# A two-layer decode kernel: second-layer P.V with V moving, another order in the last round, and another closing MLP

## The chip, the cores and the metric

The kernel runs on one core of a Trainium2 chip. The metric is the device time of one execution in microseconds (us), lower is better. The core has five engines with queues of their own: PE (TensorE; its weight loads are shown apart as PEld), DVE (VectorE), ACT (ScalarE), POOL (GpSimd) and SP (SyncE), which here only issues DMAs. They wait for each other by semaphores.

## What is computed

Two identical decoder layers in sequence, for 8 sequences of one new token each, both layers over the same K and V cache and with the same weights:

```python
def _A_ref(x, k_cache, v_cache, wq, wo):          # x: 8 x 1 x 512
    q = (x @ wq).reshape(B, 1, 32, 128).transpose(0, 2, 1, 3)
    k = jnp.repeat(k_cache, 4, axis=1)            # cache: 8 x 8 heads x 8192 x 128
    v = jnp.repeat(v_cache, 4, axis=1)
    p = _softmax(jnp.einsum("bhqd,bhkd->bhqk", q, k) * 128 ** -0.5)
    o = jnp.einsum("bhqk,bhkd->bhqd", p, v)
    return o.transpose(0, 2, 1, 3).reshape(B, 1, 4096) @ wo

def _B_ref(x, w1, w2):                            # 512 -> 1792 -> 512
    return _silu(x @ w1) @ w2

x = x + _A_ref(_layernorm(x), k_cache, v_cache, wq, wo)
x = x + _B_ref(_layernorm(x), w1, w2)
x = x + _A_ref(_layernorm(x), k_cache, v_cache, wq, wo)
x = x + _B_ref(_layernorm(x), w1, w2)
```

All inputs are bf16. K and V of one sequence and one KV head are 2 MB each; the 64 of them make 134 MB of K and 134 MB of V, and both layers need all of it.

## The kernel before

**Tasks.** A task is (layer, batch b, KV head g): 128 in all. Its 8192 keys are cut into 4 granules of 512 KB (k = 0 to 3) of two halves each, so a task has 8 half-granules; the main loop counts them with `p`, 8 positions a task. A half-granule is 8 chunks of 128 keys.

**The arena.** `ARENA` holds 28 slots of one granule (512 KB). For heads 3 to 7 (`first` = 3) the K granules of the batch in turn stay in 20 home slots from the first-layer task to the second-layer task, transposed: such a *kept* second-layer task loads only V and transposes no K. Everything else streams through the slots that are free.

**The order.** `make_tasks` writes it: per batch b the five kept first-layer tasks, then `HIDE` = 4 other tasks (first-layer tasks of later batches, second-layer tasks of heads 0 to 2 of earlier ones), in whose shadow the chain of batch b runs (wo, layer norm, w1, silu, w2, layer norm, wq: `chain_of`), then the five kept second-layer tasks `c[b]`, then what is left of that round. In the last round (b = 7) all of the other tasks stand ahead of `c[7]`, and the three second-layer tasks of heads 0 to 2 of batch 7 close the kernel. `plan_loads` then makes a list of loads, of 1, 2 or 4 granules by the table `WIDTHS` and by how tight the slots are, each with a slot and the position after which it may be issued; SP issues them in that order, each waiting for its slot.

**One position** (loop at the end of `_build`), in the order of emission: `emit_q` at the end of the task before; `emit_t` for position p + 1 (K not kept: 8 transposes on PE into a PSUM bank, and one copy of 128x1024 back into the arena, on ACT for the half-granules in `ACT_EVAC` and on DVE for the others); at odd p `emit_s`, the scores of a granule: four products of 512 columns, each with 32 output rows, into the four quarters of one PSUM bank; at even p `emit_pv` for two half-granules 12 positions back. The softmax of a task runs in the first positions of the next one: position 0 the maximum (DVE, POOL), 1 the shift and the exponential (DVE, ACT, into `P`), 3 the sum and `emit_pt` (four transposes of P on PE, one DVE copy into `PT`), 7 the reciprocal. P.V begins at position 4. `emit_norm` multiplies the result by the reciprocal, 18 positions after the task's first.

**P.V before** (`emit_pv`): V is the stationary operand. Each chunk of 128 keys is loaded as weights (128x128) and a few columns of `PT` move through it, repeated to 64 (heads 3 to 7) or 48 columns; 64 such products a task accumulate in a PSUM bank `OTp`, whose columns are then the wanted 128 (features) x 4 (query heads).

**The closing.** When the last task is done, `closing` does batch-wide wo residual, layer norm, MLP and the output: means by PE (`means`), x minus mean into `xbB` (DVE), w1 on that (`project`), squares and their sum over partitions (ACT, DVE, POOL), the inverse root by Ln and Exp on ACT, a table load (`load_table(SILU)`), the scaling (DVE), silu (ACT), w2 on PE into the bank that already holds x, a copy to `P`, and four output DMAs. `keep_busy` issues products whose result nobody reads.

Of the kernel before, what the change touches and what calls it, by code (L numbers as in the profile page):

```python
# [13 lines left out]
GRP = 8  # L14
GPT = 8
# [10 lines left out]
HIDE = 4  # L26
WIDTHS = {
# [35 lines left out]
SILU = 18  # L63
ACT_EVAC = (1, 4, 6)

# [105 lines left out]
def make_tasks(nb, nkv, keep_from):  # L171
# [11 lines left out]
    for b in range(nb):  # L183
        if b:
            tasks += kept[b]
        size = -(-(2 * first * (nb - 1)) // nb) if b in (0, nb - 1) else 2 * first * (nb - 1) // nb
        must = max(0, first * min(b + 1, nb - 1) - na)
        nd = size if b == nb - 1 else min(len(behind), first, size - must)
        more = behind[:nd] + ahead[na:na + size - nd]
        del behind[:nd]  # L190
        na += size - nd
        if b + 1 == nb:
            more += behind
        hide = len(more) if b + 1 == nb else HIDE
        tasks += more[:hide] + c[b] + more[hide:]
        behind += d[b]
# [14 lines left out]
def plan_loads(tasks, kept, nslot, ngran):  # L211
# [29 lines left out]
    def phase(i):  # L241
        if i >= len(tasks) - ENDING:
            return None
# [4 lines left out]
        if j < 0:  # L248
            return None
# [78 lines left out]
def _build(ctx, nc, A_x, A_k_cache, A_v_cache, A_wq, A_wo, B_w1, B_w2, out):  # L328
# [29 lines left out]
    def sb(shape, dt, name):  # L358
        _cnt[0] += 1
        return ctx.enter_context(nc.sbuf_tensor(f"{name}_{_cnt[0]}", shape, dt))  # L360
# [38 lines left out]
    PT = PTb[:, :].rearrange("p (x q) -> p x q", q=NQ * USED)  # L399
# [3 lines left out]
    small = sb([128, 4 * B + 4 * REP * NST + USED + 2 * FT + 2 * HQ + NST + 1 + halves], FP32, "small")  # L403
    taken = [0]
# [91 lines left out]
    with nc.Block() as block:  # L496

        @block.sync
        def _(sync_eng):
# [29 lines left out]

            queue = list(loads)  # L530
# [23 lines left out]

            evacs = [0]
# [11 lines left out]
            def emit_t(i):  # L567
# [11 lines left out]
                if i % GPT in ACT_EVAC:  # L579
# [69 lines left out]
            def emit_pt(ti):  # L649
# [9 lines left out]
                    PT.rearrange("p x (c q) -> p x c q", q=USED),  # L659
                    tpv.rearrange("p x (c q) -> p x c q", q=QUAD)[:, :, :, 0:USED]),  # L660
# [6 lines left out]
            def emit_pv(i):  # L667
# [4 lines left out]
                pv = PT.rearrange("p x (c r k) -> p x c k r", c=NQ, k=NGRAN)  # L672
# [12 lines left out]

            def width_of(ti):
                return PVN[(tasks[ti][2], NGRAN - 1) in kept]

            def emit_norm(ti):
# [4 lines left out]
                else:  # L694
                    dst, rd = QA[:, b * HQ + g * REP:b * HQ + (g + 1) * REP], f"QA{b}"
                op(dve, lambda: dve.tensor_tensor(dst, OTp[ob][:, 0:REP * width_of(ti):width_of(ti)], rcp[st], ALU.mult),
                   reads=[f"OT{ob}", f"rcp{st}"], writes=[rd])
# [119 lines left out]
            def closing(x0, x1, r0, r1):  # L817
# [3 lines left out]
                def quads(lhs_of, rhs_of, parts, first, last):  # L821
# [5 lines left out]
                        for k in range(parts) for c in range(KT)  # L827
# [6 lines left out]
                mm_group(quads(lambda k, c: x1[:, c, :], lambda k, c: ident[:, :], 1, True, False),  # L834
                         reads=[r1, "ident"], writes=["SC0"])
# [4 lines left out]
                   reads=["s1"], writes=["s1a"])  # L840
                op(dve, lambda: dve.scalar_tensor_tensor(
                    xbB, means[:, 0:B].unsqueeze(1).to_broadcast([128, KT, B]), -1.0 / D, x1, op0=ALU.mult, op1=ALU.add),
                   reads=["SC1", r1], writes=["PT", "xb"])
                project(w1_sb, "w1", range(FT), KT, lambda k: xbB[:, k, :], "xb", B, again=AGAIN)[0]()
                keep_busy(AFTER)
# [7 lines left out]
                load_table(SILU)  # L853
                scaled(hB.rearrange("p (f b) -> p f b", b=B), ["P"], FT, AGAIN)
                op(act, lambda: act.activation(hsB, hB, ACT.Silu), reads=["P"], writes=["hsB"])
# [106 lines left out]
            LQ = 1  # L962
            soft = {0: [softmax_max], 1: [softmax_shift, softmax_exp], 3: [softmax_sum, emit_pt], 7: [softmax_rcp]}
# [12 lines left out]
            ntask = len(tasks)  # L976

            for p in range(NG + LP + GPT + 1):
# [36 lines left out]
                if done >= 0 and done % GPT == 0 and done // GPT < ntask:  # L1015
                    tj = done // GPT
                    emit_norm(tj)
# [52 lines left out]
```

## Time and profile before

| what | value |
|---|---|
| time, median of 3 runs | 1159.66 us (1158.61 to 1160.57) |
| the profiled execution: its time | 1162.76 us |
| the profiled execution: its span (first to last instruction) | 1161.0 us |
| busy: PE / PEld / DVE / ACT / POOL | 83% / 66% / 51% / 33% / 10% of the span |
| moved by DMA | 467.96 MB, 403 GB/s on the mean |
| chain that ended last, by engine | DMA 55%, PE 33%, DVE 4%, ACT 3% |
| mean granted PE clock | 0.956 |

Groups that the change touches, as the page lists them (line, engine, operation, shapes and count; busy us, mean ns of one; idle time before, with what ended it): the products of `emit_pv` (L679), 8192 in all, are busy 321.1 us with 191 ns on the mean; those of `emit_s` (L613), 2048, 213.1 us and 404 ns; the copy into `PT` (L658), 128, 37.3 us and 291 ns; the copies of K on ACT (L580), 264, 267.1 us and 1012 ns; `emit_norm` (L696), 128 of about 152 ns.

How to read it: a busy time is the time in which at least one instruction of the group was running; products on PE overlap, so 191 ns is the length of one from start to end and not the spacing. "Idle before" of an engine that has nothing to do costs nothing. In a timeline line the first number is the start in us from the first instruction, the second the length, and what stands in brackets is how long the engine sat idle before and who released it. Chains name the last thing waited for.

### The profile page before, as it was taken

The numbers are of one execution on the slowest core, as the hardware profiler recorded it, in microseconds if no ns is written. First come the engines' busy times: TensorE is split into PE (matmuls) and PEld (weight loads), VectorE is DVE, ScalarE is ACT, GpSimd is POOL, SyncE is SP. The second block draws the span as 40 slices with busy tenths as digits, with TensorE's granted clock in tenths as the row PEclk, the third lists the DMA queues.
The fourth block names the chain that finished last, engine by engine and source line by source line (L and its number), as shares of the span: only waits on it lengthen the run. The fifth ranks groups of instructions, "written<-read, shape, count | busy, mean of one in ns | idle before, by whom it ended". The sixth has DMA issues, their size and how long they took to land.

```text
span 1161.0 us, 44754 instructions
## 1 busy us (share of the span) xinstructions
PE 969.4 (83%) x19900; PEld 762.2 (66%) x19904; DVE 595.4 (51%) x1936; ACT 387.9 (33%) x663; POOL 117.3 (10%) x299
## 2 busy tenths in 40 slices
PE   4688888898879887889789888898789887898787
PEld 3476766677657765677567766676567666677566
DVE  3345654556445554556445654556355554556434
ACT  1233322343134332443134422343144322343223
POOL 0000010001101011001100110001100011011010
PEclk8789998999989999999989998899999989999999
DMA  9999999999999999999999999999999999999996
GB/s 365 387 422 409 397 414 423 420 395 399 416 423 416 354 409 426 421 402 403 422 422 409 392 412 426 410 399 407 423 417 414 368 390 425 422 391 408 410 414 239
DMA packets 87137, 467.96 MB, mean 403 GB/s; under 512 B 9112, under 2 KB 13216, under 8 KB 63776
## 3 DMA queue, kind: packets, MB, share of 16 engines
q1 hardware_dynamic: 86896, 465.08, 99.0%
q8 instruction: 157, 2.57, 0.9%
q14 instruction: 36, 0.29, 0.1%
q10 hardware_dynamic: 48, 0.01, 0.0%
HBM read 465.05 MB, written 0.01 MB: 401 GB/s over the span
## 4 chain that ended last, share of the span: by engine, by line
DMA 55%; PE 33%; DVE 4%; ACT 3%; issue 3%; SPq 2%; POOL 1%; POOLq 0%; ACTq 0%
DMA arena<-in_A_k_cache_dram 40%; DMA arena<-in_A_v_cache_dram 14%; PE TPp L574 13%; PE OTp L679 9%; PE SCp L613 6%; PE MISC L780 3%; SPq L468 2%; PE TPp L654 2%; ACT arena L580 1%; ACT P L638 1%; PE MISC L799 1%; DVE small L624 1%; DVE PT L658 1%; POOL small L628 1%; DVE arena L582 1%
## 5 line engine op out<-in xcount | busy, mean ns | idle before, releaser
L574 PE MATMUL TPp<-ident,arena 128*128 128x128 bf16 x5632 | 453.3, 226 | 91.2 <-DMA arena<-in_A_k_cache_dram 87.1
L582 DVE COPY arena<-TPp 128x1024 bf16<-128x1024 bf16 x440 | 304.1, 691 | 310.3 <-PE TPp L574 309.2
L574 PEld LDWEIGHTS TPp<-ident,arena 128*128 128x128 bf16 x5632 | 338.7, 101 | 153.7 <-DMA arena<-in_A_k_cache_dram 99.0
L580 ACT COPY arena<-TPp 128x1024 bf16<-128x1024 bf16 x264 | 267.1, 1012 | 441.7 <-PE TPp L574 441.1
L679 PE MATMUL OTp<-PT,arena 128*128 128x64 bf16 (+1 forms) x8192 | 321.1, 191 | 37.9 <-DMA arena<-in_A_v_cache_dram 17.1
L679 PEld LDWEIGHTS OTp<-PT,arena 128*128 128x128 bf16 x8192 | 278.7, 99 | 73.8 <-issue 46.5
L613 PE MATMUL SCp<-arena,QB 128*32 128x512 bf16 x2048 | 213.1, 404 | 17.6 <-ACT arena L580 11.1
L638 ACT ACTIVATE P<-SCp,small 128x512 bf16<-128x512 f32 x128 | 87.9, 687 | 222.1 <-DVE small L634 155.5
L628 POOL PARTITION_ALL_REDUCE small<-small x128 | 47.5, 371 | 691.6 <-DVE small L626 658.4
L613 PEld LDWEIGHTS SCp<-arena,QB 128*32 128x32 bf16 x2048 | 55.9, 94 | 67.5 <-DVE small L626 14.9
L624 DVE TENSOR_REDUCE small<-SCp 128x1 f32<-128x512 f32 x128 | 85.7, 670 | 22.6 <-PE SCp L613 21.9
L658 DVE COPY PT<-TPp 128x256 bf16<-128x256 bf16 x128 | 37.3, 291 | 88.8 <-PE TPp L654 88.7
L646 POOL PARTITION_ALL_REDUCE small<-small x128 | 55.9, 436 | 265.5 <-DVE small L644 265.5
L654 PE MATMUL TPp<-ident,P 128*128 128x128 bf16 x512 | 51.3, 223 | 22.1 <-ACT P L638 21.9
L654 PEld LDWEIGHTS TPp<-ident,P 128*128 128x128 bf16 x512 | 29.1, 98 | 54.6 <-ACT P L638 36.0
L780 PE MATMUL MISC<-XT,wq 128*128 128x32 bf16 x1024 | 41.2, 178 | 0.8 <-issue 0.8
L605 ACT COPY QB<-QT 128x4 bf16<-128x4 bf16 x64 | 12.9, 201 | 85.7 <-DVE QT L915 85.7
L780 PEld LDWEIGHTS MISC<-XT,wq 128*128 128x128 bf16 x1024 | 32.9, 96 | 10.6 <-issue 10.6
L644 DVE TENSOR_SCALAR small<-small 128x4 f32<-128x4 f32 x128 | 28.7, 224 | 19.8 <-ACT P L638 19.5
L894 DVE SCALAR_TENSOR_TENSOR small<-small,MISC 128x4 f32<-128x4 f32 (+1 forms) x64 | 13.9, 218 | 45.6 <-PE MISC L780 45.2
L799 PE MATMUL MISC<-at,wo 128*128 128x32 bf16 x1024 | 34.6, 176 | 0.5 <-issue 0.5
L799 PEld LDWEIGHTS MISC<-at,wo 128*128 128x128 bf16 x1024 | 31.0, 96 | 4.4 <-issue 3.1
(79 smaller groups left out, 342.4 us busy)
## 6 DMA issues: line engine op xcount, KB each, us to landing
arena<-in_A_v_cache_dram SPq DMA_DIRECT2D x240, 512.0 KB, 8.1
arena<-in_A_v_cache_dram SPq DMA_DIRECT2D x90, 1024.0 KB, 12.4
arena<-in_A_k_cache_dram SPq DMA_DIRECT2D x40, 2048.0 KB, 16.4
arena<-in_A_k_cache_dram SPq DMA_DIRECT2D x144, 512.0 KB, 8.1
arena<-in_A_v_cache_dram SPq DMA_DIRECT2D x23, 2048.0 KB, 14.2
arena<-in_A_k_cache_dram SPq DMA_DIRECT2D x24, 1024.0 KB, 10.6
wq<-in_A_wq_dram SPq DMA_DIRECT2D x1, 4096.0 KB, 16.8
wo<-in_A_wo_dram SPq DMA_DIRECT2D x1, 4096.0 KB, 27.9
```

Source lines behind the costliest of these rows:

```text
L574: lambda c=c: pe.transpose(tpv[:, c, :], chunk(slot, h * GRP + c), ident[:, :])
L580: op(act, lambda: act.copy(dst, TPp[tb][:, :]), reads=[f"TP{tb}"], writes=[r_half(slot, h)])
L582: op(dve, lambda: dve.tensor_copy(dst, TPp[tb][:, :]), reads=[f"TP{tb}"], writes=[r_half(slot, h)])
L613: lambda c=c: pe.matmul(SCp[bank][c * QUAD:(c + 1) * QUAD, :], QB[qn][:, NGRAN - 1 - k:NGRAN - 1 - k + QUAD], ARENA[:, slot * SLOT + c * K ...
L624: op(dve, lambda: dve.tensor_reduce(rowmax, SCp[bank][:, :], AX.X, ALU.max), reads=[f"SC{bank}"], writes=["rowmax"])
L628: op(pool, lambda: pool.partition_all_reduce(tops, top, 128, bass.bass_isa.ReduceOp.max), reads=["top"], writes=["tops"])
L638: op(act, lambda: act.activation(P[:, :], SCp[bank][:, :], ACT.Exp, bias=shift, scale=SM_SCALE, accum_out=rs[st]), reads=[f"SC{bank}", "sh ...
L646: op(pool, lambda: pool.partition_all_reduce(ssa[st], ssm[st], 128, bass.bass_isa.ReduceOp.add), reads=[f"ssm{st}"], writes=[f"ssa{st}"])
L654: lambda c=c: pe.transpose(tpv[:, c, :], P[:, c * 128:(c + 1) * 128], ident[:, :])
L679: lambda c=c, cc=cc: pe.matmul(otp, chunk(slot, h * GRP + c), pv[:, cc % CPB, cc // CPB % NQ, k, :].unsqueeze(2).to_broadcast([128, REP, w ...
L780: lambda i=i, o=o, k=k: pe.matmul(MISC[:, i * n:i * n + w] if again == 1 else MISC[:, i * w:(i + 1) * w].rearrange("p (r b) -> p r b", b=n ...
L799: lambda o=o, h=h: pe.matmul(MISC[:, o * w:(o + 1) * w], wo_sb[:, h, o * 128:(o + 1) * 128], rhs_of(h).to_broadcast([128, w]) if n == 1 el ...
```

## The change

Four things, in one diff.

1. **P.V of the kept second-layer tasks** (`tiled`): now PT is the stationary operand (16 columns: 4 chunks x 4 query heads) and V moves, 512 columns (4 chunks x 128 features) a product. There are two products a half-granule, each with its own quarter of the output rows; over the four granules they accumulate. Of each 16 x 512 block only the four 4 x 128 blocks on the diagonal are wanted. `gather` copies half of the bank (256 float32 columns) to SBUF with ACT, twice; `turned` multiplies each 128-column piece, in float32, with a matrix of zeros and ones (`pick`), which picks the rows, sums the four quarters and turns the result to features x query heads, in a score bank that is free at that time. `emit_norm` reads it there, at position 7 of the task instead of position 2 (`SPLIT` = 3: copy, product, copy, product at positions 3, 4, 5, 6). `PT` gets another layout, for all tasks. The K copies on ACT of the two tasks after a tiled one are those of half-granules 1, 4, 7 instead of 1, 4, 6.
2. **The last round**: only four tasks stand ahead of `c[7]`, as in the other rounds; the other two, (1, 6, 1) and (1, 6, 2), come after it. With that the planner's list changes from its 512th entry on: 553 loads instead of 564 (512 KB: 368 instead of 384; 1 MB: 116 instead of 114; 2 MB: 66 instead of 63).
3. **The closing**: w1 runs on x itself, and the mean is taken off afterwards with the column sums of w1 (`col1`, which the kernel has already); silu is h / (1 + exp(-h)), with Exp on ACT and the sum, the reciprocal and the product on DVE; the table load is gone.
4. `phase` gives names (`last1`, `start1`, ...) where it gave None; `WIDTHS` has no entry under these names, so no load changes by that.

```diff
+LASTHIDE = 4
...
-SILU = 18
 ACT_EVAC = (1, 4, 6)
+XW = 4
+SPLIT = 3
+TILED_EVAC = (1, 4, 7)
...
-        hide = len(more) if b + 1 == nb else HIDE
+        hide = LASTHIDE if b + 1 == nb else HIDE
...
+    pick = sb([128, XW * REP], FP32, "pick")
...
+            op(dve, lambda: dve.tensor_reduce(
+                    pick[:, :], ident[:, :].rearrange("p (c q) -> p q c", q=QUAD)[:, 0:XW * REP, :], AX.X, ALU.add), ...)
+            for n in range(2):
+                op(dve, lambda n=n: dve.memset(OTp[n][:, :], 0.0), writes=[f"OT{n}"])
...
-                if i % GPT in ACT_EVAC:
+                if i % GPT in (TILED_EVAC if i // GPT >= 2 and tiled(i // GPT - 2) else ACT_EVAC):
...
-                    PT.rearrange("p x (c q) -> p x c q", q=USED),
-                    tpv.rearrange("p x (c q) -> p x c q", q=QUAD)[:, :, :, 0:USED]),
+                    PT.rearrange("p (c k x r) -> p x c r k", c=NQ, k=NGRAN, r=REP),
+                    tpv.rearrange("p x (c q) -> p x c q", q=QUAD)[:, :, :, 0:USED].rearrange("p x c (r k) -> p x c r k", k=NGRAN)),
...
+                if tiled(ti):
+                    steps = []
+                    for n in range(GRP // XW):
+                        cc = h * GRP + n * XW
+                        at = (cc // CPB * (NGRAN - 1) + k) * CPB * REP
+                        tile = h * (GRP // XW) + n
+                        steps.append(
+                            lambda cc=cc, at=at, tile=tile: pe.matmul(
+                                OTp[ob][tile * QUAD:tile * QUAD + XW * REP, 0:XW * 128],
+                                PT[:, at + cc * REP:at + (cc + XW) * REP],
+                                ARENA[:, slot * SLOT + cc * 128:slot * SLOT + (cc + XW) * 128],
+                                start=(k == 0), stop=(k == NGRAN - 1),
+                            )
+                        )
+                    mm_group(steps, reads=[r_half(slot, h), "PT"], writes=[f"OT{ob}"])
+                    return
...
+            def tiled(ti):
+                return tasks[ti][0] == 1 and tasks[ti][2] >= first
+
+            def gather(ti, n, _bank):
+                ob = ti % 2
+                op(act, lambda: act.copy(Pf[:, :], OTp[ob][:, n * 256:(n + 1) * 256]), reads=[f"OT{ob}"], writes=["P"])
+
+            def turned(ti, n, bank):
+                mm_group(
+                    [lambda x=x: pe.matmul(SCp[bank][:, 0:REP], Pf[:, (x % 2) * 128:(x % 2 + 1) * 128],
+                                           pick[:, x * REP:(x + 1) * REP], start=(x == 0), stop=(x == XW - 1))
+                     for x in (2 * n, 2 * n + 1)], reads=["P", "pick"], writes=[f"SC{bank}"])
...
 # closing
+                project(w1_sb, "w1", range(FT), KT, lambda k: x1[:, k, :], r1, B, again=AGAIN)[0]()
+                mm_group(quads(lambda k, c: x1[:, c, :], lambda k, c: ident[:, :], 1, True, False), ...)
+                keep_busy(AFTER)
                 op(dve, lambda: dve.scalar_tensor_tensor(
-                    xbB, means[:, 0:B].unsqueeze(1).to_broadcast([128, KT, B]), -1.0 / D, x1, op0=ALU.mult, op1=ALU.add), ...)
-                project(w1_sb, "w1", range(FT), KT, lambda k: xbB[:, k, :], "xb", B, again=AGAIN)[0]()
-                keep_busy(AFTER)
+                    ev, means[:, 0:B].unsqueeze(1).to_broadcast([128, FT, B]), -1.0 / D,
+                    col1.unsqueeze(2).to_broadcast([128, FT, B]), op0=ALU.mult, op1=ALU.mult), ...)
...
-                load_table(SILU)
-                scaled(hB.rearrange("p (f b) -> p f b", b=B), ["P"], FT, AGAIN)
-                op(act, lambda: act.activation(hsB, hB, ACT.Silu), reads=["P"], writes=["hsB"])
+                op(dve, lambda: dve.tensor_tensor(hv, MISC[...], ev, ALU.add), ...)
+                op(dve, lambda: dve.tensor_tensor(hv, hv, yr[...], ALU.mult), ...)
+                op(act, lambda: act.activation(ehB, hB, ACT.Exp, scale=-1.0), reads=["P"], writes=["eh"])
+                op(dve, lambda: dve.tensor_scalar(ehB, ehB, 1.0, None, op0=ALU.add), ...)
+                op(dve, lambda: dve.reciprocal(ehB, ehB), reads=["eh"], writes=["eh"])
+                op(dve, lambda: dve.tensor_tensor(hsB, hB, ehB, ALU.mult), ...)
...
 # main loop
+            parts = XW // 2
+            rows_at = {SPLIT + 2 * n + m: (f, n) for n in range(parts) for m, f in enumerate((gather, turned))}
+            finish = SPLIT + 2 * parts
...
-                if done >= 0 and done % GPT == 0 and done // GPT < ntask:
-                    tj = done // GPT
-                    emit_norm(tj)
+                tj, d = done // GPT, done % GPT
+                split = 0 <= tj < ntask and tiled(tj)
+                bank = (tj + 1) % NSCP if split else None
+                if split and d + GPG in rows_at:
+                    f, n = rows_at[d + GPG]
+                    f(tj, n, bank)
+                if 0 <= tj < ntask and d == (finish - GPG if split else 0):
+                    emit_norm(tj, bank)
```

## The prediction

> **What bounds the kernel now.** I read the slices of the page first. The DMA row shows the 16 DMA engines busy from the first slice to the last but one:
>
> ```profile
> DMA  9999999999999999999999999999999999999996
> GB/s 365 387 422 409 397 414 423 420 395 399 416 423 416 354 409 426 421 402 403 422 422 409 392 412 426 410 399 407 423 417 414 368 390 425 422 391 408 410 414 239
> ```
>
> 465 MB have to come in; at 425 GB/s, the best slices, they would take 1094 us, at the mean 403 GB/s 1154 us of the 1161.0 us span. Next I read the sums of three stretches of one round (batch 1's turn; the columns are length, busy time of PE, PEld, DVE, ACT and POOL, granted clock, DMA share, GB/s): the first-layer tasks that refill the kept K, the four full tasks ahead of the kept second-layer ones, and the five kept second-layer tasks themselves ("c-tasks" from here on):
>
> ```profile
> 319.00:380.00 61.00, 51.14 (x971) 40.89 (x972) 30.35 (x80) 23.95 (x39) 5.23 (x13) 0.94 1.01 420
> 380.00:424.00 44.00, 38.58 (x800) 30.90 (x796) 26.76 (x98) 16.11 (x27) 4.79 (x12) 0.96 0.98 372
> 424.00:449.00 25.00, 21.00 (x509) 15.15 (x504) 11.29 (x49) 4.20 (x13) 3.58 (x9) 1.00 1.02 418
> ```
>
> The DMA share is 1.01 and 1.02 in the first and last; it falls only in the middle one. So the c-tasks, the ones this change speeds up or slows down, run while the DMA engines have no room left. What PE does after them is in the waits of PE by stretch (us in total, times, longest), here 319 to 380 us and then 710 to 767 us:
>
> ```profile
> PE TPp L574 <- DMA arena<-in_A_k_cache_dram: 6.4, 3, 4.2
> PE OTp L679 <- DMA arena<-in_A_v_cache_dram: 1.4, 2, 1.0
> ...
> PE TPp L574 <- DMA arena<-in_A_k_cache_dram: 3.3, 1, 3.3
> ```
>
> After each set of c-tasks PE catches up with its data and waits: 9.1, 7.8, 7.7, 8.3, 3.3, 6.8 and 7.4 us in the seven rounds that have such a stretch (the same two rows, each round). This is the slack that a slower c-task may use up, and why a quicker one gains nothing: PE would wait longer for the same bytes. Last, the pace of a c-task, PE alone, near the end (start, length, what):
>
> ```profile
> 1106.31 0.40 PE L613 MATMUL SCp<-arena,QB 128*32 128x512 bf16 x4
> ...
> 1109.47 0.40 PE L654 MATMUL TPp<-ident,P 128*128 128x128 bf16 x4 [0.96 <-ACT P L638]
> 1109.71 0.72 PE L799 MATMUL MISC<-QA,wo 128*128 128x8 bf16 x16
> 1110.35 0.63 PE L679 MATMUL OTp<-PT,arena 128*128 128x64 bf16 x16
> 1110.90 0.40 PE L613 MATMUL SCp<-arena,QB 128*32 128x512 bf16 x4
> 1111.23 0.64 PE L679 MATMUL OTp<-PT,arena 128*128 128x64 bf16 x16
> 1111.81 0.40 PE L613 MATMUL SCp<-arena,QB 128*32 128x512 bf16 x4
> ```
>
> From last scores to last scores 5.50 us. 3.2 of them are the softmax (from the scores at 1106.31 to the turning of P at 1109.47); PE has finished its other work by then and waits 0.96 us.
>
> **P.V with V moving.** Per c-task 64 products of 64 columns (16 take 0.55 to 0.58 us: 1110.35 to 1110.90, 1111.23 to 1111.81) become 16 of 512 columns in four groups of 32 output rows, the form of the scores, whose four take 0.33 us (1110.90 to 1111.23). Four such steps save 0.24 each, 0.95 us of PE. But two of the four lie inside the softmax's 3.2 us, ahead of a wait; only the two behind the turning of P shorten the loop: -0.47 us a task.
>
> **Picking the blocks.** Per c-task ACT copies 128x256 float32 twice; between 128x4 (0.20 us) and 128x1024 (1.01 us), so about 0.4 us each, on an engine busy 4.2 of 25 us there. PE turns them in four float32 products, two after P.V step 4 and two after step 6, both in the loop. No row has a float32 product. From below: a weight load and product of bf16 in a stream, 0.035 us (16 in 0.55). From above: the two unoverlapped (99 ns load, 176 ns product of 32 columns, L799), doubled because the elements have twice the bytes: 0.55 us. I take 0.28, the pair once, since only two come together and little overlaps: 4 x 0.28 = +1.12 us a task (0.14 to 2.2). New waits: the first turning waits for ACT's first copy, which starts when the turning of P has read P (1109.7) and is over by about 1110.3 with handing over, while PE is in P.V until 1110.7; ACT's second copy waits for the first turning (P is one buffer), 0.4 + 0.2 us, while PE does scores and P.V, 0.66 us. Behind either on PE stand the next scores, and the softmax behind those; I count 0, and 0.3 us a task if the cover is gone. The norm comes some five half-granules later and only feeds a result that is needed at the end.
>
> The copy of P's transpose, 291 ns for 128x256, now writes with a stride in all 128 tasks, and P.V waits for it: 0 if its row stands; its upper end is one element where the rows have two (691 ns for 1024 elements and 291 for 256 give 0.52 ns each): +0.13 us. I take 0, the row of the same shape.
>
> The Trainium skill (VectorE: DVE Perf Modes, "Mode 2×_1P") wants a step of one for two 16-bit elements a cycle; by it the copy would take 0.13 us more, an estimate that the two rows above bear out in the slope but not in the stride. By it the sum below would be 0.65 us a round higher, still under the slack.
>
> Sum per c-task: -0.47 + 1.12 = +0.65 us (-0.33 to +2.2 with everything), 3.3 us a round. The smallest slack is 3.3, the others 6.8 or more. So 0 on the end, by cover of PE's waits for DMA; without that cover 7 x 3.3 = 23 us.
>
> **The last round.** The c-tasks of batch 7 move ahead of two full tasks (161, 162), so five full tasks close the kernel and not three, with the kept slots free for them. The planner's list then holds 368 loads of 512 KB and not 384, the difference in larger ones. 512 KB pieces run at 408 GB/s (1060 to 1087 us), larger ones at 426 (960 to 980 us): 8.39 MB x (1/408 - 1/426) = -0.9 us. From 1125.95 us to the end PE waits for no DMA in the chain: it is a little late. With 8.1 us of PE work a task (scores at 1133.75 and 1141.85) against 4.19 MB / 408 = 10.3 us of transfer, five tasks give it time to catch up: the last P.V can follow its data, 0 to -0.75 us; I take -0.4.
>
> **The closing.** What falls out and comes in:
>
> ```profile
> 1155.58 0.21 ACT L852 ACTIVATE small<-small 128x8 f32<-128x8 f32 x1
> 1155.80 1.28 ACT L513 ACT_TABLE_LOAD   x1
> 1156.16 0.27 DVE L755 TENSOR_TENSOR P<-MISC,small 128x112 f32<-128x112 f32 x1 [0.86 <-PE MISC L780]
> 1157.10 0.30 ACT L855 ACTIVATE PT<-P 128x112 bf16<-128x112 f32 x1
> 1157.44 0.77 PEld L823 LDWEIGHTS SCp<-w,PT 128*8 128x8 bf16 x56 [1.16 <-ACT PT L855]
> ```
>
> Before: the root at 1155.79, table, silu, w2 at 1157.44. After: w1 starts on raw x some 0.5 us sooner and is done before the root; then a chain: product 0.27, Exp 0.30, +1 0.2, reciprocal, product 0.27, handing over 0.05 five times. Reciprocal of 128x4 takes 169 ns (L665), of 128x14 241 (L906): 7.2 ns an element, 0.95 us for 112; from below 0.27, as any DVE op of that size (L755). With 0.95, 1155.86 + 2.25 = 1158.1: +0.7 us (0 to +0.7); I take +0.7. At the start DVE makes a mask and clears two banks, under 1.6 us (0.22 of L523, twice at most 0.69 of L582), hidden: DVE is free from 17.3 us and waits for POOL's first sum at 19.94.
>
> Sum: -0.9 - 0.4 + 0.7 = -0.6 us; span 1161.0 to 1160.4, the profiled 1162.8 to 1162.2. That execution lies 3.1 us above the median 1159.7, so: **1159.1 us**.
>
> **Rivals.** *PE becomes the bound (slower).* If a float32 product costs 0.55 us, a c-task grows by 2.2 - 0.47 + 0.13 = 1.9 us, 9.3 a round; less the slacks that leaves 0.2 + 1.5 + 1.6 + 1.0 + 6.0 + 2.5 + 1.9 = 15 us: 1174. It decides from 0.67 us a task in the tightest round, from 1.8 in all. For it: the picks sit in the serial loop. Against: five rounds have twice the slack.
>
> *Four passes.* If each float32 product is four separate pairs of 0.275 us, it costs 1.1 us, a task +4.0, a round 20: 7 x 20 - 50.4 = 90 us, 1249. As four pairs in a stream it is 0.14 and changes nothing. The Trainium skill (FP8 and Floating Point Precision, "TensorE Precision Notes") says that true FP32 takes four passes through the array; no run here shows it yet.
>
> *Fewer late loads (faster).* In 13 windows of 10 us (first 40 us and the end left out) the rate falls under 390 GB/s (313 at 390 us, 322 at 900, 360 at 1030): against 408, 13.6 us lost. If less PE work lets slots come free sooner there, half may come back: 1152.3. Against: PE waits for DMA between the c-tasks and every such dip, so it arrives at the same time.
>
> *Starved last round (slower).* K of 161 and 162 are asked as 2 MB at once, for which four slots must be free; one such transfer late is 5 us (2.10 MB / 0.42): 1164. Against: 20 kept slots come free just then.
>
> **How the numbers follow.** Transfers bound, as forecast: 0.55. PE bound 0.21, four separate passes 0.04, starved round 0.05, fewer late loads 0.15. A measurement here tells 0.2% (2.3 us) from no change; of the 0.55, 0.36 lie within, 0.11 below and 0.08 above. Faster 0.11 + 0.15 = 0.26; same 0.36; slower 0.08 + 0.21 + 0.04 + 0.05 = 0.38. The range, 1152 to 1176, takes in all cases but the separate passes and the far ends of two; the likeliest one's own is 1156 to 1162.
>
> **What would show it.** Right: DMA row and GB/s as before; c-tasks of 5.5 to 6.5 us; PE's waits for DMA after them shorter by some 3 us a round; reciprocal near 0.95 us; no table load near the end. Wrong: the float32 products near 0.5 us or more and those waits near zero (PE bound), or a DMA share under 1 in the last 60 us, or the dips gone.

## The result, and the profile after

The changed kernel takes 1240.41 us (median of 6 runs, 1236.24 to 1244.24) against 1159.13 us of the kernel before (6 runs). The ratio is 1.0692 [1.0674, 1.0711]: 81 us slower, where no change was forecast and the range ended at 1176. The profiled execution took 1236.24 us, with a span of 1234.5 us. The medians and ratios below leave out two slow executions, one of 2649 us in e3 and one of 1203.62 us in e12.

First the slices of the page after: the granted clock of PE in tenths, the busy share of the DMA engines, and their rate.

```profile
PEclk8799977999789996999689986999699976998699
DMA  9999999999999997999989999999989998999991
GB/s 365 391 418 409 390 407 397 352 365 408 388 386 379 379 418 315 423 370 382 418 341 379 379 417 378 377 368 397 393 360 382 403 404 354 374 371 409 427 408 74
```

Four slices before the last show a DMA share of 7 or 8, and in 18 of the 40 the rate is under 380 GB/s (in 4 before): the transfers no longer set the end all the time. And PE's clock is at 6 or 7 tenths in 11 slices, where the kernel before has one. Next, what PE waits for, in the kernel after and then in the kernel before (us in total, times, longest; the rows that matter here).

```profile
PE OTp L709 <- DVE PT L672: 51.9, 62, 1.4
PE OTp L694 <- DVE PT L672: 41.6, 32, 1.4
...
PE TPp L588 <- DMA arena<-in_A_k_cache_dram: 20.7, 24, 5.3
...
PE OTp L709 <- DMA arena<-in_A_v_cache_dram: 3.0, 3, 1.3
```

```profile
PE TPp L574 <- DMA arena<-in_A_k_cache_dram: 87.1, 89, 5.6
...
PE OTp L679 <- DMA arena<-in_A_v_cache_dram: 17.1, 26, 1.8
PE OTp L679 <- DVE PT L658: 15.7, 33, 0.5
```

The waits for data, 87.1 + 17.1 = 104 us, have shrunk to 24; the waits for the copy of P's transpose have grown from 16 to 93 us. (L672 after is L658 before; L588, L694 and L709 are the turning of K, the tiled P.V and the old P.V.) The costliest groups that the change touches, after, with busy us and mean ns of one:

```profile
L709 PE MATMUL OTp<-PT,arena 128*128 128x48 bf16 (+1 forms) x5632 | 217.7, 189 | 72.7 <-DVE PT L672 51.9
...
L672 DVE COPY PT<-TPp 128x256 bf16<-128x256 bf16 x128 | 157.6, 1231 | 78.1 <-PE TPp L668 77.7
...
L694 PE MATMUL OTp<-arena,PT 128*16 128x512 bf16 x640 | 82.6, 505 | 51.6 <-DVE PT L672 41.6
...
L725 PE MATMUL SCp<-pick,P 128*128 128x4 f32 x320 | 65.4, 310 | 0.0
L721 ACT COPY P<-OTp 128x256 f32<-128x256 f32 x80 | 29.9, 373 | 102.5 <-PE SCp L725 86.8
```

The copy has the same shape as before, 128x256 bf16, and takes 1231 ns; it took 291. That is 0.94 us in each of 128 tasks, 120 us on DVE. The 160 float32 products show as 320 records: two loads and two products each. Here is what a kept second-layer task (a "c-task") has become on PE, part of its timeline (start, length, what; in brackets how long PE sat idle before, and for whom):

```profile
455.95 0.40 PE L668 MATMUL TPp<-ident,P 128*128 128x128 bf16 x4 [0.99 <-ACT P L652]
457.76 0.61 PE L694 MATMUL OTp<-arena,PT 128*16 128x512 bf16 x4 [1.41 <-DVE PT L672]
458.29 1.02 PE L725 MATMUL SCp<-pick,P 128*128 128x4 f32 x4
459.24 0.62 PE L627 MATMUL SCp<-arena,QB 128*32 128x512 bf16 x4
459.79 0.62 PE L826 MATMUL MISC<-XT,wq 128*128 128x32 bf16 x16
460.34 0.60 PE L694 MATMUL OTp<-arena,PT 128*16 128x512 bf16 x4
460.87 1.02 PE L725 MATMUL SCp<-pick,P 128*128 128x4 f32 x4
```

Two things stand out. Behind the turning of P, PE sits idle for 1.41 us until the copy is done. And then everything is slow: the four products of the scores last 0.62 us, where the prediction's timeline of before had 0.40. The stretch that this lies in (columns: length, busy PE, PEld, DVE, ACT, POOL, clock, DMA share, GB/s) was granted a clock of 0.73; the first-layer tasks behind it get 0.95, but their transfers run at 351 GB/s:

```profile
440.00:478.00 38.00, 27.63 (x412) 15.99 (x412) 16.75 (x53) 6.88 (x21) 4.01 (x10) 0.73 1.01 422
478.00:545.00 67.00, 59.67 (x1037) 45.70 (x1030) 40.38 (x92) 28.91 (x48) 5.60 (x14) 0.95 0.88 351
```

In the first of the prediction's three rows, the same kind of stretch (319 to 380 us), the rate was 420; in its third, the c-tasks, the clock was 1.00. The closing is this, on DVE and ACT:

```profile
1228.49 0.28 DVE L901 TENSOR_TENSOR P<-MISC,P 128x112 f32<-128x112 f32 x1 [0.33 <-PE MISC L826]
...
1229.11 0.30 ACT L906 ACTIVATE P<-P 128x112 f32<-128x112 f32 x1 [0.47 <-DVE P L904]
...
1229.69 0.85 DVE L908 RECIPROCAL P<-P 128x112 f32<-128x112 f32 x1
```

From the last norm to the output's DMA it takes 6.54 us (1225.69 to 1232.23), before 5.90 (1152.87 to 1158.77): +0.6.

**By tasks.** Each task copies its queries into QB once, so the distance from one such copy to the next is the pace of a task. Summed over 124 tasks (the first three and the last left out), by kind:

| | 40 c-tasks | 40 first-layer tasks that refill the kept K | 44 others | span |
|---|---|---|---|---|
| before | 212 us (5.30 each) | 386 | 488 | 1161.0 |
| after | 302 us (7.54 each) | 374 | 480 | 1234.5 |

The c-tasks lose 90 us; the others give back only 20, since they too wait for the copy now. 90 - 20 = 70 of the 73.5 us by which the span grew.

### The profile page after: what moved, and what is told of

The parts are those of the page before. It is cut to its first block, busy times and chain, and to the rows that moved or that the text cites. A ratio compares the mean times of both kernels' runs of the same rounds, so it can differ in the third digit from the quotient of the medians.

```text
span 1234.5 us, 41708 instructions
## 1 busy us (share of the span) xinstructions
PE 1017.7 (82%) x18304; PEld 747.7 (61%) x18304; DVE 701.4 (57%) x1943; ACT 415.3 (34%) x742; POOL 117.3 (9%) x299
## 4 chain that ended last, share of the span: by engine, by line
PE 58%; DVE 16%; DMA 13%; ACT 6%; issue 4%; SPq 3%; POOL 1%; ACTq 0%; DVEq 0%
PE TPp L588 19%; PE SCp L627 12%; DVE PT L672 12%; DMA arena<-in_A_k_cache_dram 11%; PE OTp L709 9%; PE SCp L725 5%; PE OTp L694 4%; ACT arena L594 4%; PE TPp L668 4%; PE MISC L826 3%; SPq L472 2%; ACT P L652 2%; DVE small L638 1%; DMA arena<-in_A_v_cache_dram 1%; PE MISC L845 1%
## 5 line engine op out<-in xcount | busy, mean ns | idle before, releaser
L588 PE MATMUL TPp<-ident,arena 128*128 128x128 bf16 x5632 | 448.8, 225 | 24.3 <-DMA arena<-in_A_k_cache_dram 20.7
L596 DVE COPY arena<-TPp 128x1024 bf16<-128x1024 bf16 x440 | 315.0, 716 | 263.2 <-PE TPp L588 261.7
L588 PEld LDWEIGHTS TPp<-ident,arena 128*128 128x128 bf16 x5632 | 340.3, 101 | 87.0 <-issue 62.2
L709 PE MATMUL OTp<-PT,arena 128*128 128x48 bf16 (+1 forms) x5632 | 217.7, 189 | 72.7 <-DVE PT L672 51.9
L709 PEld LDWEIGHTS OTp<-PT,arena 128*128 128x128 bf16 x5632 | 191.0, 98 | 96.5 <-issue 90.5
L627 PE MATMUL SCp<-arena,QB 128*32 128x512 bf16 x2048 | 230.2, 439 | 21.8 <-ACT arena L594 15.0
L672 DVE COPY PT<-TPp 128x256 bf16<-128x256 bf16 x128 | 157.6, 1231 | 78.1 <-PE TPp L668 77.7
L694 PE MATMUL OTp<-arena,PT 128*16 128x512 bf16 x640 | 82.6, 505 | 51.6 <-DVE PT L672 41.6
L638 DVE TENSOR_REDUCE small<-SCp 128x1 f32<-128x512 f32 x128 | 86.2, 673 | 11.2 <-PE SCp L627 11.0
L725 PEld LDWEIGHTS SCp<-pick,P 128*128 128x128 f32 x320 | 58.8, 259 | 28.6 <-issue 15.9
L725 PE MATMUL SCp<-pick,P 128*128 128x4 f32 x320 | 65.4, 310 | 0.0
L721 ACT COPY P<-OTp 128x256 f32<-128x256 f32 x80 | 29.9, 373 | 102.5 <-PE SCp L725 86.8
L694 PEld LDWEIGHTS OTp<-arena,PT 128*16 128x16 bf16 x640 | 17.6, 92 | 68.0 <-issue 63.1
```

Of the source, the lines that this page charges most:

```text
L588: lambda c=c: pe.transpose(tpv[:, c, :], chunk(slot, h * GRP + c), ident[:, :])
L596: op(dve, lambda: dve.tensor_copy(dst, TPp[tb][:, :]), reads=[f"TP{tb}"], writes=[r_half(slot, h)])
L627: lambda c=c: pe.matmul(SCp[bank][c * QUAD:(c + 1) * QUAD, :], QB[qn][:, NGRAN - 1 - k:NGRAN - 1 - k + QUAD], ARENA[:, slot * SLOT + c * K ...
L638: op(dve, lambda: dve.tensor_reduce(rowmax, SCp[bank][:, :], AX.X, ALU.max), reads=[f"SC{bank}"], writes=["rowmax"])
L672: op(dve, lambda: dve.tensor_copy(PT.rearrange("p (c k x r) -> p x c r k", c=NQ, k=NGRAN, r=REP), tpv.rearrange("p x (c q) -> p x c q", q= ...
L694: lambda cc=cc, at=at, tile=tile: pe.matmul(OTp[ob][tile * QUAD:tile * QUAD + XW * REP, 0:XW * 128], PT[:, at + cc * REP:at + (cc + XW) * ...
```

## The experiments

Two theories stood against each other at first: that the copy with its new order of writing costs the time (the first, A), and that the float32 products do (B). The times are medians, and the ratio is to the kernel before in the same session (its medians lay between 1159.56 and 1159.99). The columns on the c-tasks come from the profile of each run, over the eight stretches from the first c-task's copy into QB to that of the task behind the last (423.72 to 449.29 us is one of them in the kernel before). "Clock" is the granted clock, weighted by their length. "Columns" are what PE moves in 3.41 us, each weighted by the width of the product's weights; the last section says how and why.

| run | time, us | ratio [95%] | copy, ns | c-task, us | clock in c-tasks | PE busy share there | columns there | PE waits for DMA, us |
|---|---|---|---|---|---|---|---|---|
| before | 1159.13 | | 291 | 5.30 | 0.98 | 0.81 | 4120 | 104 |
| after | 1240.41 | 1.0692 [1.0674, 1.0711] | 1231 | 7.54 | 0.70 | 0.73 | 2150 | 24 |
| e1: new copy alone | 1179.46 | 1.0168 [1.0137, 1.0200] | 1232 | 6.21 | 0.91 | 0.74 | 3500 | 26 |
| e2: after, copy in order of destination | 1161.72 | 1.0018 [1.0004, 1.0033] | 425 | 6.39 | 0.80 | 0.78 | 2560 | 60 |
| e3: after, copy in runs of 16 | 1160.53 | 1.0000 [0.9984, 1.0017] | 292 | 6.11 | 0.85 | 0.79 | 2660 | 62 |
| e4: after without picks | 1174.94 | 1.0124 [1.0104, 1.0145] | 1231 | 5.73 | 0.83 | 0.69 | 2670 | 26 |
| e5: e3 without picks | 1157.99 | 0.9989 [0.9975, 1.0002] | 292 | 4.85 | 0.95 | 0.73 | 3180 | 116 |
| e8: e3 with picks doubled | 1192.06 | 1.0283 [1.0264, 1.0301] | 291 | 7.15 | 0.73 | 0.84 | 2290 | 46 |
| e9: after, wait filled | 1189.65 | 1.0280 [1.0252, 1.0308] | 1235 | 6.74 | 0.97 | 0.77 | 3200 | 23 |
| e11: slow copy in c-tasks only | 1196.86 | 1.0317 [1.0297, 1.0336] | 1226 / 425 | 7.32 | 0.71 | 0.75 | 2220 | 40 |
| e12: slow copy elsewhere only | 1191.62 | 1.0237 [1.0202, 1.0271] | 425 / 1234 | 6.75 | 0.72 | 0.79 | 2400 | 23 |

### The new copy alone

The kernel before, with nothing but the new layout of PT, the copy that writes it, and the old P.V reading it:

```diff
-    PT = PTb[:, :].rearrange("p (x q) -> p x q", q=NQ * USED)
+    PT = PTb[:, :]
...
-                    PT.rearrange("p x (c q) -> p x c q", q=USED),
-                    tpv.rearrange("p x (c q) -> p x c q", q=QUAD)[:, :, :, 0:USED]),
+                    PT.rearrange("p (c k x r) -> p x c r k", c=NQ, k=NGRAN, r=REP),
+                    tpv.rearrange("p x (c q) -> p x c q", q=QUAD)[:, :, :, 0:USED].rearrange("p x c (r k) -> p x c r k", k=NGRAN)),
...
-                pv = PT.rearrange("p x (c r k) -> p x c k r", c=NQ, k=NGRAN)
+                pv = PT.rearrange("p (c k x r) -> p x c k r", c=NQ, k=NGRAN, r=REP)
```

> The kernel before with one thing of the change alone: the new layout of PT and its copy (each element written 16 elements from the last). P.V, the last round and the closing are as before. Theory A (the copy is the cause): the copy takes 1.2 us as in the changed kernel, PE waits for it in every task, a first-layer task goes from 8.2 to about 8.9 us, and the time rises by most of the 81 us, to 1205 to 1235. Theory B (the float32 picks and the PE clock are the cause): the copy may be long, but it hides behind PE's waits for DMA, and the time stays under 1170.

Measured 1179.46 us, between what the two theories gave: the copy is no trifle, and it isn't the whole. PE's waits in this run:

```profile
PE OTp L679 <- DVE PT L658: 93.5, 96, 1.4
PE TPp L574 <- DMA arena<-in_A_k_cache_dram: 20.2, 25, 4.7
...
PE OTp L679 <- DVE small L665: 10.7, 9, 1.4
PE OTp L679 <- DVE small L894: 6.7, 7, 1.0
PE OTp L679 <- DMA arena<-in_A_v_cache_dram: 6.1, 7, 2.5
PE OTp L679 <- DVE small L704: 5.5, 7, 0.8
```

The wait for the copy is as long as in the kernel after (93.5 us), and the waits for data have fallen by as much as it has grown: 104 to 26 us, and 16 to 93.5. PE also waits 23 us for small work of DVE (L665, L894, L704) for which it had waited 0.5 us before. So the copy alone uses up nearly all of the slack and comes out 20 us over it. Whatever comes on top after that has little left to hide in.

### The same layout, written in another order

What is it in the copy that is slow: the layout, or the order of writing? Only the order of the two access patterns is changed, so that the destination is written from front to back and the source is read with steps:

```diff
-                    PT.rearrange("p (c k x r) -> p x c r k", c=NQ, k=NGRAN, r=REP),
-                    tpv....rearrange("p x c (r k) -> p x c r k", k=NGRAN)),
+                    PT.rearrange("p (c k x r) -> p c k x r", c=NQ, k=NGRAN, r=REP),
+                    tpv....rearrange("p x c (r k) -> p c k x r", k=NGRAN)),
```

> The changed kernel with the same layout of PT, but the copy runs in the order of the destination: it writes one after the other and reads PSUM in steps (k of stride 1 outside, x of 128, r of 4 elements). If the strided write is what costs, the copy falls to 0.29 to 0.45 us and under theory A the time to 1160 to 1185. If any copy that is not in runs on both sides costs, it stays at about 1.2 us and the time at 1240. Theory B: about 1230 whatever the copy does.

```profile
L672 DVE COPY PT<-TPp 128x256 bf16<-128x256 bf16 x128 | 54.4, 425 | 86.5 <-PE TPp L668 86.3
```

Measured 1161.72 us: 79 of the 81 us are gone with one line, the same bytes in the same places. 425 ns is 291 plus 0.13 us, the prediction's upper end, which it had reckoned as one element moved where the row of before moves two. The remaining 0.8 us up to 1231 come from the writing: in the changed kernel the source is read in a row and the innermost index of the destination steps by 16 elements, 32 bytes, at each element.

### Runs of 16 elements

The layout itself is changed: copies of 16 elements in a row, and the tiled P.V takes every fourth element as its stationary operand.

```diff
-                    PT.rearrange("p (c k x r) -> p x c r k", c=NQ, k=NGRAN, r=REP),
-                    tpv....[:, :, :, 0:USED].rearrange("p x c (r k) -> p x c r k", k=NGRAN)),
+                    PT.rearrange("p (c x q) -> p x c q", c=NQ, q=USED),
+                    tpv....[:, :, :, 0:USED]),
...
-                                PT[:, at + cc * REP:at + (cc + XW) * REP],
+                                PT.rearrange("p (y k) -> p y k", k=NGRAN)[:, cc * REP:(cc + XW) * REP, k],
```

> The changed kernel with PT in another layout, quarter, chunk, head, granule: the copy writes runs of 16 elements, and the weights of the tiled products take every fourth element. The copy should take 0.29 us as before the change. Theory A: 1158 to 1175, as the prediction had it without the copy. Theory B: 1220 or more.

```profile
L672 DVE COPY PT<-TPp 128x256 bf16<-128x256 bf16 x128 | 37.3, 292 | 89.2 <-PE TPp L668 89.2
```

292 ns, and 1160.53 us: with the copy at its old price the rest of the change comes out even with the kernel before, as the prediction had it for the whole. Its c-task grows by 6.11 - 5.30 = 0.81 us (predicted 0.65).

### Without the picks, and with twice as many

In two runs `gather` and `turned` are left out, so the second layer's kept part of the result isn't computed; the norm reads a corner of the P.V bank. One is the kernel after, the other the version in runs of 16:

```diff
-                    src, rs_ = SCp[bank][:, 0:REP], f"SC{bank}"
+                    src, rs_ = OTp[ob][:, 0:REP], f"OT{ob}"
...
-                    f(tj, n, bank)
+                    pass
```

> The changed kernel without the picking: the two ACT copies and the four float32 products of a kept second-layer task are left out, and the norm reads a corner of the bank of P.V (so the second layer's result is not the reference's). The slow copy of PT stays. Theory A: the first-layer tasks stay at 8.95 us, and the time at 1200 to 1225. Theory B: within 15 us of the kernel before, under 1175.

> The kernel with the copy in runs, without the picking (ACT copies and float32 products left out, so the second layer's result is not the reference's): the shortest kept second-layer tasks of all, some 5 us. DMA bound: 1158 to 1161. If the new P.V itself could bring anything, this is where it would show: under 1155.

1174.94 and 1157.99 us. With the slow copy the picks are worth 65 us (1240.4 - 1174.9), with the quick one 3 (1160.5 - 1158.0). The first run came out where theory B had put it and not A, while the two with a quick copy came out where A had them. So neither theory holds alone: take away the slow copy or the picks, and most of the 81 us go. The same four products cost nothing while PE would wait for data anyway, and their price or more once it doesn't. In the second run PE's waits for data are longer than before the change, and the time does not fall with them: the transfers set the end there.

```profile
PE TPp L588 <- DMA arena<-in_A_k_cache_dram: 90.2, 71, 6.6
```

For the price of the picks themselves, each float32 product is issued twice, in the version in runs of 16 (the mask is halved, so that the sum stays):

```diff
+            op(dve, lambda: dve.tensor_scalar(pick[:, :], pick[:, :], 0.5, None, op0=ALU.mult), ...)
...
-                      for x in (2 * n, 2 * n + 1)], ...)
+                      for x in (2 * n, 2 * n + 1) for m in range(2)], ...)
```

> The kernel with the copy in runs (e3_runs), with each float32 product done twice (the matrix holds 0.5, so the result stays). A theory of a shared slack: the costs of the change are paid out of PE's waits for DMA (62 us left in e3_runs, some 40 of them in the main part) and only the rest is seen. Doubling adds 160 products of 0.27 us at full clock to 0.48 at half, 43 to 76 us of PE: the waits fall to 20 to 30 us, and the time rises to 1165 to 1200. If the picks cost nothing on the end however long (DMA bound throughout), 1161.

1192.06 us. The c-task grows by 7.15 - 6.11 = 1.04 us for four products more, 0.26 each; the first four cost 6.11 - 4.85 = 1.26, with the copies and waits that belong to them. The prediction had taken 0.28 each. 40 x 1.04 = 42 us on PE lengthen the kernel by 32; some of it came out of PE's waits for data, which fall from 62 to 46 us (20 to 30 us had been expected). So B's part is real, and it is the price that was foreseen, but it shows only without slack.

### The two small parts

The closing alone, in the kernel before (`w1` on raw x, silu by Exp and reciprocal; the hunk "closing" of the diff and nothing else), and the last round alone:

```diff
-        hide = len(more) if b + 1 == nb else HIDE
+        hide = HIDE
```

> The kernel before with the new closing alone (w1 on raw x, silu by an exponential). From the profile of the changed kernel, whose closing takes 6.5 us from the last norm to the output DMA where it took 5.9: +0.6 us, a ratio of 1.0005, not to be told from no change. A rival, that the table load was also in the way of something else, would give 1 us or more off.

> The kernel before with the new order of the last round alone. The prediction had it at -1.3 us (larger pieces -0.9, a last P.V that follows its data -0.4), a ratio of 0.9989. The rival, a starved last round, gives +5 us, 1.004.

1159.60 us, 1.0003 [0.9993, 1.0014], and 1159.59 us, 0.9997 [0.9987, 1.0007]. Neither can be told from no change. Neither has a part in the 81 us that could be seen.

### The clock

The stretch at 440 us had a clock of 0.73. To see what that costs, the wait for the copy in the c-tasks is filled with four products of 512 columns that nobody reads (L608; the profile shows three of them):

```diff
+                    if ph == 3 and ti + 1 < ntask and tiled(ti + 1):
+                        keep_busy(4)
```

> The changed kernel, slow copy and all, with four idle products of 512 columns put behind the turning of P in the kept second-layer tasks, where PE waits 1.41 us for the slow copy. If half of the price in these tasks is the PE clock, which falls after that wait (scores 0.62 us long for 0.40, a pair of float32 products 0.95 us for 0.53), it stays up, a task falls from 8.2 to about 7 us, and the time from 1240 to 1190 to 1215. If the clock falls for another reason, or matters little, 1235 to 1245.

1189.65 us, 51 less than the kernel after, by adding work. The timeline of a c-task, and the stretch that answers to 440 to 478:

```profile
447.36 0.40 PE L668 MATMUL TPp<-ident,P 128*128 128x128 bf16 x4 [0.98 <-ACT P L652]
447.81 0.81 PE L608 MATMUL TPp<-wq,ident 128*128 128x512 bf16 x3
449.18 0.39 PE L694 MATMUL OTp<-arena,PT 128*16 128x512 bf16 x4 [0.56 <-DVE PT L672]
449.50 0.61 PE L725 MATMUL SCp<-pick,P 128*128 128x4 f32 x4
450.04 0.40 PE L627 MATMUL SCp<-arena,QB 128*32 128x512 bf16 x4
```

```profile
438.00:470.00 32.00, 25.91 (x370) 14.55 (x373) 16.18 (x49) 7.88 (x22) 3.57 (x9) 0.95 1.02 422
```

P.V still starts 1.8 us after the turning of P (457.76 - 455.95 and 449.18 - 447.36): the copy is as slow as it was. But the scores are back at 0.40 us, and two float32 products take 0.54 us (449.50 to 450.04) where they took 0.95 (458.29 to 459.24). The clock over all c-tasks goes from 0.70 to 0.97, the task from 7.54 to 6.74 us. In the profiled spans that is 32 of the 49 us gained; 16 more lie in the 44 other tasks.

The same filling (two products) in the version in runs of 16, which would be a way to beat the kernel before:

> The kernel with the copy in runs (e3_runs) and two idle products behind the turning of P in the kept second-layer tasks, the best version that the runs so far point to. If the DMA engines bound it, a quicker kept task (6.1 to about 5.7 us) gives nothing: 1158 to 1161, the same as the kernel before. If the dips of the DMA rate came from PE being late, it would come out 3 us or more under it.

1159.86 us, 1.0003 [0.9990, 1.0015]: nothing, because PE isn't what sets the end there. No version came out ahead of the kernel before.

### Where the slow copy costs

The copy is slow in all 128 tasks. In the first of two runs it is written in the slow order in the 40 c-tasks alone, and in the order of the destination (425 ns) in the others; the second is the converse.

```diff
+                if tiled(ti):
                     op(dve, lambda: dve.tensor_copy(
                         PT.rearrange("p (c k x r) -> p x c r k", ...),
...
+                else:
+                    op(dve, lambda: dve.tensor_copy(
+                        PT.rearrange("p (c k x r) -> p c k x r", ...),
...
```

> The changed kernel with the slow copy only for the 40 kept second-layer tasks; the other 88 copy in the order of the destination (0.43 us). Shared slack: the kept tasks stay at 7 to 7.6 us, but first-layer tasks can run at 8.2 to 8.4 us again and take back some 0.5 us each: 1190 to 1220. If the price sits in the kept tasks alone, 1230 to 1240.

> The other way about: the slow copy in the 88 other tasks, the quick one in the 40 kept ones. Shared slack: kept tasks at 6.4 us as in e2_dst_order, first-layer tasks no faster than 8.95 us: 1170 to 1195. If the price sits in the kept tasks alone, 1160 to 1165.

1196.86 and 1191.62 us (the second from 1184 to 1200). Against 1161.72 with the quick order everywhere, the slow copy costs 35 us in the c-tasks alone and some 30 in the others alone (22 to 38). Together they cost 79, some 14 more than the sum, which is no surer than the spread of the second run. The c-tasks pay as much with 40 copies as the others with 88. Part of that goes with the clock, 0.71 in the c-tasks of the first run against 0.80 with the quick order. The others pay because their copy stands on PE's path too: in the second run PE waits 51.8 us for it there, and its waits for data are down to 23 us.

The two kinds aren't quite apart. A task's copy runs while the next task has its turn, so in the second run one slow copy a round falls into the first c-task. Of the 33 us by which its profiled span exceeds that of the quick order (1198.4 against 1165.2), 14 lie in the c-tasks, which take 6.75 us and not the 6.4 that had been expected.

## Why the prediction was wrong, step by step

**What bounds the kernel before: right.** The c-tasks were run at 4.85, 5.24 (the closing alone), 5.30, 6.11 and 6.39 us, and the time stayed between 1158.0 and 1161.7.

**P.V with V moving: right.** Predicted -0.47 us a task. With the slow copy it is 5.73 - 6.21 = -0.48 (without picks, against the copy alone), with the quick one 4.85 - 5.30 = -0.45. The clocks within each pair are a little lower with the new form: 0.83 against 0.91, 0.95 against 0.98.

**The picks: right, as long as the copy is quick.** Predicted 0.28 a product and 1.12 a task, measured 0.26 and 1.04 to 1.26; ACT's copy 373 ns for the 0.4 taken. With the slow copy they cost 7.54 - 5.73 = 1.81 us a task, and the clock goes from 0.83 to 0.70 with them.

**The copy of P's transpose: the step that failed.** The prediction took it at 0, "the row of the same shape", with an upper end of +0.13 us. It is +0.94. The shape wasn't the thing to go by: the diff changed the order in which the elements are written, and the row that it went by writes them one after the other. What was called an upper end was the price of one possible loss, that of pairs, and the run in order of the destination comes out at just that (425 ns). The other loss, of the step, was not bounded at all. By the prediction's slope a copy of no elements takes 158 ns, so it is (1231 - 158) / 256 = 4.2 ns an element against 0.52.

The trace of before had a row for it, under another operation. At the start of the kernel `scaled` (L755) writes 256 bf16 elements from PSUM into `QA` with a step of 32 elements, 64 bytes (`QAv`); in the closing the same line writes 112 float32 elements in a row:

```profile
L755 DVE TENSOR_TENSOR QA<-MISC,small 128x256 bf16<-128x256 f32 x1 | 1.3, 1267 | 0.2 <-PE MISC L780 0.2
...
L755 DVE TENSOR_TENSOR P<-MISC,small 128x112 f32<-128x112 f32 x1 | 0.3, 273 | 0.9 <-PE MISC L780 0.9
```

1267 ns is (1267 - 158) / 256 = 4.3 ns an element by the same reckoning. An upper end taken from this row would have been +0.98 us a copy, 125 us over 128 tasks.

The prediction weighed the rule of pairs; the one that fits what ran is elsewhere in the Trainium skill (Advanced Engine Details and Errata, "SBUF Cachelines"): a line has 16 bytes, and full speed needs at least two accesses to a line. Steps of 32 and of 64 bytes meet a new line each time, and they cost 4.2 and 4.3 ns an element here; runs of 16 elements and the order of the destination don't, and both are quick. No run has a step of 4 to 16 bytes in the destination, so the length of the line isn't shown.

**The sum per c-task:** predicted +0.65 us, measured +0.81 with the copy at its old price and +2.24 with the slow one. Of the 1.43 between these two, 0.94 is the copy. The other 0.5 I put down to the clock (0.70 against 0.85), which the sum didn't have at all; filling the wait, with the copy as slow as ever, took 0.80 off.

**The cover:** the slack of 50.4 us behind the c-tasks was read rightly, but only the c-tasks were set against it. The copy is in all tasks, and 128 x 0.94 = 120 us of it stood against the 104 us in which PE waited for data anywhere. With the copy at zero that sum was never made. (Not all of it is seen as waits: PE's wait for the copy grows by 78 us.) By the prediction's own rule 2.24 us a task would have been 11.2 a round, 28 us over the slacks; the runs with the slow copy in one kind of task or the other show that the 88 others cost about as much as the c-tasks, 30 us for 35.

**The last round and the closing:** predicted -1.3 and +0.7 us. The intervals allow -1.5 to +0.8 and -0.8 to +1.6; the trace shows +0.6 for the closing and a reciprocal of 0.85 for 0.95. Nothing contradicts them, and they are too small to be told.

**The rivals.** "PE becomes the bound" is what happened, with a cause that it did not have: its price was to come from float32 products at 0.55 us, and these took 0.27. Its sign was right, its 1174 us was not. "Four passes" is refuted as it was meant: each product shows as two pairs and not four, 0.27 us together at full clock; that its 1249 lies near the result is chance. It is at half the clock that two of them take 0.95 us, close to that rival's price of one. "Fewer late loads" didn't come (the rate fell), and would not have paid much: without picks and with more slack than before, the time was 1157.99 us, a ratio of 0.9989 [0.9975, 1.0002], not to be told from no change. "Starved last round" is refuted by the last round alone.

**What stays open.** That the wait for the copy and the picks lower the clock in the c-tasks is shown by runs that differ in one of them; why they do is only narrowed down, by a count over the traces (below). And some 14 of the 79 us that the slow copy costs (6 to 22, by the spread of the second run) are a joint effect of both kinds of task that no run takes apart.

## What to carry to other kernels

When a diff permutes an access pattern, write down for each side the step of the innermost index in bytes before taking the price of a row with the same shape, and look for a row with the same kind of step, whatever its operation: the order of writing alone made this copy four times as long, and one line of it was worth 79 us. Before a cost is set against a slack, list every loop that draws on the same slack, and do it with the upper end of each cost: here the copy alone cost 20 us and all the rest alone nothing, and together they cost 81. If an engine's wait sits beside work that suddenly takes half as long again, look at the granted clock of that stretch first; filling the wait is a cheap test.

## What the runs showed of the hardware

- **Writing with steps of 32 or 64 bytes cost DVE 4.2 to 4.3 ns an element.** 256 bf16 elements from PSUM to SBUF: 1231 ns with 32-byte steps in the destination (1267 with 64-byte steps, another operation), 425 with 8-byte steps in the source and a packed destination, 292 with runs of 16 on both sides. A read with 32-byte steps wasn't run.
- **The granted clock doesn't follow the busy share of PE.** In the c-tasks of three runs PE was busy 0.73 to 0.74 of the time, at clocks of 0.95 (e5: tiled P.V, no picks, quick copy), 0.91 (e1: old P.V, slow copy) and 0.70 (after). With the picks doubled it was busy 0.84 of the time at 0.73. The wait for the copy lowers the clock in every pair: from 0.98 to 0.91 with the old P.V, from 0.95 to 0.83 with the tiled one without picks, from 0.85 to 0.70 with picks. The picks lower it too, from 0.95 to 0.85 and from 0.83 to 0.70. The Trainium skill (TensorE: Matmul & The Clock Gate, "What's actually happening") gives an idle window of some 3.4 us for the clock to be halved; no wait in these stretches is longer than 1.9 us, so here that rule by itself doesn't say when it happens.
- **It goes with the columns that move, weighted by the width of the weights.** In every trace here the clock is 1.0 or 0.5 and holds for whole multiples of 3.41 us. For each such window of the eleven profiles in the table, the columns that the products of the profile move were added up: in full where the weights are 128 columns wide, a quarter for the scores (32), an eighth for the tiled P.V (16). Under a sum of 2200, 367 of 371 windows were followed by one at half the clock; from 3400 up, 3 of 2827; between them 185 of 544. The best single limit on the sum (2816) tells the next clock rightly for 3614 of these 3742 windows, the best one on PE's busy share for 3388. A slow clock itself moves fewer columns, but among windows at full clock it is the same: 146 of 149, and 3 of 2716. A c-task moves 6390 such columns before and 4750 after, in longer time; a float32 product of the picks moves only 4, a wait none, and the filling products of e9 are 128 wide. This is a count over traces; no run varied the width of the weights alone.
- **Waiting can cost more than working.** Four products in a wait of 1.4 us in each c-task (the profile shows three of them), read by nobody, took 51 us off 1240.
- **A float32 product of 128x128 with 4 columns** is two loads and two products in the profile, 0.27 us at full clock and 0.48 at half.
